# Attention products as 64x64 weights in the four quarters of the array, and float32 x of the last nine tiles for the sums of blocks

## Chip, cores and metric

The kernel runs on one core of one Trainium2 chip. The metric is the device time of one execution in microseconds (us). PE is the matrix engine (TensorE), DVE the vector engine, ACT the scalar engine, POOL the GpSimd engine, and SP the engine that issues the DMA transfers. A line number such as L895 is one of the kernel before.

## What is computed

A linear attention without softmax (4 batches, 8 heads, 576 tokens, 64 columns), then a gated feed-forward block, then a second block with a softmax-like gate and a layer norm. The sizes are 2304 tokens, 512 columns, 1536 and 1024 hidden columns.

```python
kv = einsum('bhsd,bhse->bhde', k, v)            # 64x64 for each batch and head
out = einsum('bhsd,bhde->bhse', q, kv)
x = out / sqrt(mean(out*out) + 1e-6) * g_norm   # 2304 x 512 after the heads are joined
y = ((x @ w_a) * (x @ w_b)) @ w_out             # 512 -> 1536 -> 512
h = y @ w_in                                    # 512 -> 1024
s = h * softmax(h)
result = layer_norm(s) * g_ln @ w_out2          # 1024 -> 512
```

The weights of the two blocks arrive as float64. The kernel takes each apart with integer operations and splits it into a high and a low part, and does the same with x, so that a product of near float32 accuracy is three matrix products of rounded operands.

## The kernel before

The order of all work is written by a planner that runs when the kernel is built. It keeps a clock of its own (`Order`): a step on PE has a written cost, an operation on ACT, DVE or POOL a written duration, and whatever is ready first by that clock is emitted next. Each engine then works through its list in that order and waits on the chip for what it needs. So a wait at the head of an engine's list holds all that stands behind it.

Tokens are worked in 18 tiles of 128 for the attention and in 6 blocks of 384 (three tiles each) for the first feed-forward products.

Attention. `att_kv` (L833) makes the 64x64 products k'v of a batch; ACT copies them to `bd`. `att_1` (L880) makes one tile of `out`: for each of 4 pairs of heads, 2 heads and every sequence in the tile, a product with q as the weights and `bd` as the moving operand. A sequence has 576 tokens, so tiles 4 and 13 hold two sequences and the other 16 hold one. For a tile of one sequence the weights are 64 rows by 128 columns, and there are 8 products; for a tile of two they are 64x64, and there are 16. The two heads use the upper and the lower rows of the array, and for a tile of two sequences the two halves of the tokens use the left and the right columns. After it ACT squares the tile (L933) and copies it (L935), DVE sums the squares (L923), ACT adds the epsilon, POOL takes the root, and DVE or POOL scales x (L927).

For tiles 0 to 11, `att_2` (L980) turns x on PE with four transposes; ACT writes the high part `xh` from PSUM (L994) and DVE the low part `xl` (L995). Tiles 12 to 17 go another way (`att_hop`, L939): DVE turns 32x32 blocks (L951), the tile goes to HBM and back through SP's queue (L956, L962), ACT writes a float32 tile `xs` (L965) and from it `xh` (L969), and DVE writes `xl` (L970).

First feed-forward products. `ab_items` (L1044) makes the products of the first two blocks f of 128 hidden columns, for all six blocks j of tokens: 12 units of 24 products, interleaved with the attention and then alone. The loop takes attention steps between them by a credit. Then come the "plain" units (`plain_step`, L1137) of hidden blocks 2 and 3, in three steps t of two token blocks each, 12 more units. Hidden blocks 4 to 11 are made in steps of seven products instead of eight (`step_items`, L1172), which work on sums of token blocks. `x_sums` (L1076) and `x_sum_of` (L1089) make these sums T1 to T4 for each t on DVE in PSUM banks 4 to 7 (L1098), out of the high and the low parts; T4 is written over the first half of block 2t+1, so it waits until the plain step of t is through. The sums of one t begin when those of the t before are written, and the first when all four weights of hidden blocks 2 and 3 lie in HBM.

Weights on their way: raw float64 from HBM (L381), decoded by ACT (L436) and five operations of DVE (L439 to L457), joined (L592), split (L621, L623), written to HBM (L565), and read back into their place when that is free (L686).

The names and lines that the change and the steps of the prediction touch: `w` and the loop over `bs` in `att_1` (L886 to L896), `xs_t` (L270, L948), `att_2` (L993 to L999), `SUMS`, `x_sum_of`, and the order of steps (L1703).

Of the kernel before, what the change touches and what calls it, by code (L numbers as in the profile page):

```python
# [9 lines left out]
F32 = mybir.dt.float32  # L10
F32R = mybir.dt.float32r
# [191 lines left out]
def attention_moe_moe_kernel(ctx: ExitStack, tc, kv_in, kv_tail, q_in, g_norm, w1, w_in, w_out2, g_ln, out):  # L203
# [63 lines left out]
    W_AT = [[M.W + 14336 * m + o for o in (0, 4096, 8192, 12288)] for m in range(2)]  # L267
    yb_t = [M(f"yb{i}", [P, DM], F32, W_AT[i // 2][1] + 2048 * (i % 2)) for i in range(4)]

    xs_t = [M(f"xs{i}", [P, NP, P], F32, M.R2 + 2048 * i) for i in range(6)]  # L270


    xh = [M(f"xh{j}", [P, NP, TB], F32R, M.XB + 12288 * j) for j in range(NTB)]
# [606 lines left out]
    def att_1(t):  # L880

        sx, ss, sr = (r.take() for r in (R_X, R_SQ, R_R))
        ps, free = two_banks()
        bs = seqs(t)
        off = t * P - t * P // S * S
        w = P // len(bs)  # L886
        for p in range(NP):
            if len(bs) == 2:
                src = arrived["qs", bs[0], 0][1][:, p, :]
            else:  # L890
                src = arrived["q", bs[0], p // 2][1][:, p % 2, off - (S - 4 * P) * (bs[0] % 2):][:, 0:P]
            for m, b in enumerate(bs):
                for h in range(2):
                    hs = slice(h * D, (h + 1) * D)
                    nc.tensor.matmul(ps[m * w:(m + 1) * w, h, p * D:(p + 1) * D], lhsT=src[hs, m * w:(m + 1) * w],  # L895
                                     rhs=bds[b % 2][hs, p], start=True, stop=True)  # L896
        for b in bs:
            b_left[b] -= 1
        if len(bs) == 1 and (off >= S - P or bs[0] % 2 == 0 and off == 3 * P):
            for u in range(NP // 2):  # L900
                R_Q.give(arrived.pop(("q", bs[0], u))[0])
        loads()
        x = x_t[sx % 4]
        sq = sq_t[ss % 2]
        r = r_t[sr % 4]

        o = ps[:, :, 0:NP * D].rearrange("t h (p d) -> t h p d", d=D)
        xo, sqo = (a.rearrange("t (p h) d -> t h p d", h=2) for a in (x, sq))
        rank = 1 + t / 9

        def done(when):
            R_R.give(sr)
            if t < BY_HBM:
                back.append((when, t, x, sx))
            else:
                att_hop(t, x, sx, when)

        def rest(when):
            small = ("A", 0.22, lambda: nc.scalar.activation(out=r, in_=r, func=AF.Copy, bias=1e-6))
            if t < 3:  # L920
                small = ("V", 0.1, lambda: nc.vector.tensor_scalar(out=r, in0=r, scalar1=1e-6, scalar2=None, op0=ALU.add))
            od.chain([
                ("V", 0.68, lambda: nc.vector.tensor_reduce(out=r, in_=sq, axis=AX.X, op=ALU.add)),  # L923
                (None, 0, lambda t: R_SQ.give(ss)),
                small,
                ("G", 1.76, lambda: nc.gpsimd.tensor_tensor(out=r, in0=r, in1=mhalf[:, 0:H], op=ALU.pow)),
                ("X" if t >= X_FROM else "S", (0.69, 1.3) if t >= X_FROM else 0.69, lambda e="V": tt(e)(  # L927
                    out=x, in0=x, in1=r.unsqueeze(2).to_broadcast([P, H, D]), op=ALU.mult)),
                (None, 0, done),
            ], rank=rank, t=when)  # L930

        od.chain([
            ("A", 0.6, lambda: nc.scalar.activation(out=sqo, in_=o, func=AF.Square, scale=D ** -0.5)),  # L933
            (None, 0, rest),
            ("A", 0.58, lambda: nc.scalar.copy(out=xo, in_=o)),  # L935
            free,
        ], rank=rank - 0.5, t=od.now + od.extra + 0.9 + 0.2)

    def att_hop(t, x, sx, when):  # L939

        if not R_YB.ok():
            od.chain([(None, 0, lambda w: att_hop(t, x, sx, w))], rank=1 + t / 9, t=when + 0.2)
            return
        sy = R_YB.take()
        y = yb_t[sy % 4]
        d = dr.tile([P, DM], F32, tag=f"sx{sy % 4}", name=f"sx{t}")
        dh, dl = (a[t * P // TB][:, :, t * P % TB:t * P % TB + P] for a in (xh, xl))
        xf = xs_t[t - BY_HBM]  # L948

        def turn():  # L950
            nc.vector.transpose(out=y.rearrange("t (b p i) -> t p b i", b=4, i=32),  # L951
                                in_=x.rearrange("t h d -> t (h d)").rearrange("t (p b i) -> t p b i", b=4, i=32))

        def off(when):
            R_X.give(sx)
            nc.sync.dma_start(out=d, in_=y)  # L956
            od.chain([(None, 0, back_in)], t=max(when + 2.0, od.load(4 * P * DM)))

        def back_in(when):
            assert not kv_left[0]  # L960
            for b in range(4):
                nc.sync.dma_start(out=y[b * 32:(b + 1) * 32].rearrange("i (a e) -> i a e", a=4),  # L962
                                  in_=d.rearrange("(a i) (b e) -> b i a e", a=4, b=4)[b])
            od.chain([
                ("A", 0.68, lambda: nc.scalar.activation(  # L965
                    out=xf.rearrange("c p (a j) -> c p a j", a=4), in_=y.rearrange("c (a p j) -> c p a j", a=4, p=4),
                    func=AF.Copy, scale=gn[:, 0:1])),
                (None, 0, lambda when: R_YB.give(sy)),
                ("A", 0.58, lambda: nc.scalar.copy(out=dh, in_=xf)),  # L969
                ("S", 0.64, lambda: nc.vector.tensor_tensor(out=dl, in0=xf, in1=dh.bitcast(F32), op=ALU.subtract)),  # L970
                (None, 0, ready),
            ], rank=1 + t / 9, t=max(when + 5.2, od.load(4 * P * DM) + 1.0))

        def ready(when):
            x_ready[t] = when
            att_left[0] -= 1

        od.chain([("V", 0.69, turn), (None, 0, off)], rank=1 + t / 9, t=when)

    def att_2(t, x, sx):  # L980
        ps, free = one_bank()
        xf = x.rearrange("t h d -> t (h d)")
        for p in range(NP):
            nc.tensor.transpose(ps[:, p * P:(p + 1) * P], xf[:, p * P:(p + 1) * P], ident)  # L984
        R_X.give(sx)
        src = ps.rearrange("c (p t) -> c p t", t=P)
        dh, dl = (a[t * P // TB][:, :, t * P % TB:t * P % TB + P] for a in (xh, xl))
# [1 line left out]
        def done(when):  # L989
            x_ready[t] = when  # L990
            att_left[0] -= 1

        od.chain([  # L993
            ("A", 0.68, lambda: nc.scalar.activation(out=dh, in_=src, func=AF.Copy, scale=gn[:, 0:1])),  # L994
            ("V", 0.74, lambda: nc.vector.scalar_tensor_tensor(  # L995
                out=dl, in0=src, scalar=gn[:, 0:1], in1=dh.bitcast(F32), op0=ALU.mult, op1=ALU.subtract)),
            free,
            (None, 0, done),
        ], rank=1 + t / 9, t=od.now + od.extra + 0.46 + 0.2)  # L999
    def three(o, ah, al, bh, bl, first, last, skip=False):  # L1000
        nc.tensor.matmul(o, lhsT=ah, rhs=bh, start=first, stop=False, skip_group_check=skip)  # L1001
        nc.tensor.matmul(o, lhsT=ah, rhs=bl, start=False, stop=False, skip_group_check=skip)  # L1002
# [66 lines left out]


    x_sum = {}
    SUMS = list(range(NTB // 2))
    sum_q = list(SUMS)
    sum_banks = []

# [13 lines left out]
    def x_sum_of(t):  # L1089
        i, j = 2 * t, 2 * t + 1  # L1090
        t1, t2 = PS[:, 6:8, 0:TB], PS[:, 4:6, 0:TB]
        rank = 5.075
        (b11h, b11l), (b21h, b21l) = ([a[i][:, c:c + 2] for a in (xh, xl)] for c in (0, 2))
        (b12h, b12l), (b22h, b22l) = ([a[j][:, c:c + 2] for a in (xh, xl)] for c in (0, 2))

        def add(o, a, b, op, kind="V"):
            a, b = (v.bitcast(F32) if v.dtype == F32R else v for v in (a, b))
            return (kind, 0.98, lambda: nc.vector.tensor_tensor(out=o, in0=a, in1=b, op=op))  # L1098

        def both(n, src):  # L1100
            hi, lo = (b12h, b12l) if n == T4 else [a[t][:, (T1, T2, T3).index(n)] for a in (th, tl)]
            return [("A", 0.82, lambda: nc.scalar.copy(out=hi, in_=src)), add(lo, src, hi, ALU.subtract),
                    (None, 0, lambda w: x_sum.__setitem__((t, n), w))]

        def free(*banks):
# [4 lines left out]
        def last(w):  # L1110
# [2 lines left out]
                return  # L1113
            od.chain([*both(T4, t1), *free(6, 7)], rank=rank, t=w)

        sub = ALU.subtract
        od.chain([
            add(t1, b12h, b11h, sub, "S"), add(t1, t1, b12l, ALU.add), add(t1, t1, b11l, sub), *both(T1, t1),
            add(t2, b22h, t1, sub), add(t2, t2, b22l, ALU.add), *both(T2, t2),
            add(t1, b21h, t2, sub), add(t1, t1, b21l, ALU.add), (None, 0, last),  # L1120
            add(t2, t2, b11h, sub), add(t2, t2, b11l, sub), *both(T3, t2), *free(4, 5),
        ], rank=rank, t=od.now)


    WSEQ = [("P1", 0, 0, B11), ("P6", 1, 1, T2), ("P2", 0, 1, B21), ("P5", 1, 0, T1), ("P7", 2, 0, T3),
# [11 lines left out]
    def plain_step(fp, t):  # L1137

        items = []
        last = max(t for f, t in PLAIN_STEPS if f == fp)  # L1140
        mixed = has_group(fp, 1)
        steps_left[fp, t] = 4

# [28 lines left out]
    def step_items(fp, t):  # L1172

        st = {}
        steps_left[fp, t] = 14
        left = {(m, g): (2, 2, 2, 1)[g] for m in range(2) for g in range(4)}

        def pair_of(x):
# [20 lines left out]
        def run(m, name, g, c, n):  # L1199
# [10 lines left out]
                w = wt[m][g]  # L1210
                three(ps[:, m, 0:TB], w[:, 0, sl], w[:, 1, sl], x[2 * k], x[2 * k + 1], first and k == 0, k == 1, not first)
            left[m, g] -= 1
            if not left[m, g] and t == NTB // 2 - 1:
                slot_free[m, g] = od.now
            steps_left[fp, t] -= 1
            if m:
# [483 lines left out]

    ab = [[ab_items(f, j) for j in range(NTB)] for f in range(PLAIN)]
    busy = []
    steps = [(plain_step if (fp, t) in PLAIN_STEPS else step_items)(fp, t) for fp in range(PLAIN // 2, NF1 // 2) for t in range(NTB // 2)]  # L1703
    b_items = [x for s in steps for x in s]
    ATT, LOOK = 2.0, 4

# [168 lines left out]
```

## Time and profile before

| | |
|---|---|
| median of 3 runs | 669.76 us (669.29 to 670.35) |
| the profiled execution | 670.23 us |
| its span, first to last instruction | 668.1 us |
| PE busy | 653.9 us (98%) |
| DVE, ACT, POOL busy | 503.5, 326.5, 225.4 us |

The busy time of PE is that of matmuls which overlap one another, so it tells where PE has work and not how fast it goes. A matmul of the code leaves two records in the trace, each with a weight load: 128 products of 64x128 weights stand as 256 records. A row of the timeline that ends in x16 is 16 records run together. In the chain, each piece is work that the end of the span follows from.

### The profile page before, as it was taken

To read this page: it belongs to the slowest core of one execution; us is meant where nothing else is said; L and a number is where in the kernel's file an instruction comes from. 1 tells how busy PE (TensorE), PEld (TensorE's weight loads), DVE (VectorE), ACT (ScalarE), POOL (GpSimd) and SP (SyncE) were. 2 spreads that over 40 slices of the span, in tenths; PEclk is the share of its full clock that TensorE was granted. 3 is DMA by queue.
4 is the path that set the end of the run, shared out by engine and by line. 5 is a ranking of instruction groups with operands and counts; after the bars stand their busy time and mean duration, and the time that the engine had idled before them with its cause. 6 is when DMAs were issued, how large, how long until landed. Compare 5 with 4: busy or idle time off the path is not lost.

```text
span 668.1 us, 10827 instructions
## 1 busy us (share of the span) xinstructions
PE 653.9 (98%) x3834; PEld 597.9 (89%) x3834; DVE 503.5 (75%) x784; ACT 326.5 (49%) x563; POOL 225.4 (34%) x251
## 2 busy tenths in 40 slices
PE   5999999999999999999999999999999999999998
PEld 4889998999999999999999988888888888888887
DVE  2787789888888898888478878766379996687730
ACT  3666544334544554444345444453466765564431
POOL 1575503233331330021023323111688774452100
PEclk9999999999999999999999999999999999999999
DMA  8975589558589799799975653674604565433451
GB/s 331 381 248 176 199 259 308 205 176 317 198 311 408 289 345 350 231 394 345 403 270 154 193 165 124 223 255 151 255 0 146 160 183 158 142 112 107 129 173 48
DMA packets 93654, 150.67 MB, mean 226 GB/s; under 512 B 9504, under 2 KB 60960, under 8 KB 93600
## 3 DMA queue, kind: packets, MB, share of 16 engines
q1 hardware_dynamic: 93600, 149.98, 65.2%
q8 instruction: 30, 0.49, 0.3%
q14 instruction: 24, 0.20, 0.1%
HBM read 93.33 MB, written 56.62 MB: 224 GB/s over the span
## 4 chain that ended last, share of the span: by engine, by line
PE 94%; DMA 4%; ACT 1%; DVE 1%; SPq 0%; issue 0%; ACTq 0%; DVEq 0%
PE ps L1353 22%; PE ps L1001 18%; PE ps L1002 18%; PE ps L1003 18%; PE ps L1495 13%; PE ps L895 3%; DMA hb<-stg 1%; PE ps L852 1%; DMA kv<-in_kv 1%; DMA q<-in_q 1%; DMA wt<-hb 1%; PE ps L984 1%; PE ps L860 0%; SPq L381 0%; ACT bd L866 0%
## 5 line engine op out<-in xcount | busy, mean ns | idle before, releaser
L1353 PE MATMUL ps<-gh,wo 128*128 128x512 f32 (+1 forms) x480 | 137.5, 367 | 0.0
L1001 PE MATMUL ps<-xh,wt 128*128 128x384 f32 x384 | 129.9, 338 | 2.4 <-DMA wt<-hb 1.5
L1002 PE MATMUL ps<-xl,wt 128*128 128x384 f32 x384 | 128.4, 334 | 0.0
L1003 PE MATMUL ps<-xh,wt 128*128 128x384 f32 x384 | 128.4, 334 | 0.0
L1353 PEld LDWEIGHTS ps<-gh,wo 128*128 128x128 f32 x480 | 88.8, 188 | 11.2
L1353 PE MATMUL ps<-gl,wo 128*128 128x512 f32 (+1 forms) x240 | 88.1, 367 | 0.0
L1495 PE MATMUL ps<-bo,ao 128*128 128x512 f32 x378 | 87.5, 390 | 0.0
L1495 PEld LDWEIGHTS ps<-bo,ao 128*128 128x128 f32 x378 | 70.7, 188 | 15.1 <-ACT bt L1536 0.3
L1001 PEld LDWEIGHTS ps<-xh,wt 128*128 128x128 f32 x384 | 72.1, 188 | 3.8 <-DVE tl L1098 1.8
L1327 DVE TENSOR_TENSOR gl<-gi,gh 128x512 fp32r<-128x512 f32 (+1 forms) x60 | 45.6, 767 | 37.3 <-ACT gh L1326 37.2
L1002 PEld LDWEIGHTS ps<-xl,wt 128*128 128x128 f32 x384 | 72.1, 188 | 0.1
L1003 PEld LDWEIGHTS ps<-xh,wt 128*128 128x128 f32 x384 | 72.1, 188 | 0.0
L1326 ACT CAST gh<-gi 128x512 fp32r<-128x512 f32 (+1 forms) x60 | 34.7, 580 | 74.2 <-PE ps L1353 57.6
L1002 PE MATMUL ps<-gw,dh 128*128 128x512 f32 (+1 forms) x152 | 57.4, 378 | 0.0
L1003 PE MATMUL ps<-gw,dl 128*128 128x512 f32 (+1 forms) x152 | 57.4, 378 | 0.0
L1001 PE MATMUL ps<-gw,dh 128*128 128x512 f32 (+1 forms) x152 | 57.4, 378 | 0.0
L1040 DVE TENSOR_TENSOR g<-ps,g 128x384 f32<-128x384 f32 x72 | 39.4, 553 | 21.3 <-ACT g L1039 8.4
L1039 ACT COPY g<-ps 128x384 f32<-128x384 f32 x72 | 34.0, 482 | 41.8 <-DVE ps L1249 19.5
L1353 PEld LDWEIGHTS ps<-gl,wo 128*128 128x128 f32 x240 | 45.1, 188 | 5.5
L1001 PE MATMUL ps<-th,wt 128*128 128x384 f32 x144 | 48.3, 335 | 0.2 <-ACT s L1253 0.2
L1003 PE MATMUL ps<-th,wt 128*128 128x384 f32 x144 | 48.1, 334 | 0.0
L1002 PE MATMUL ps<-tl,wt 128*128 128x384 f32 x144 | 48.1, 334 | 0.0
(127 smaller groups left out, 1225.2 us busy)
## 6 DMA issues: line engine op xcount, KB each, us to landing
raw<-in_w SPq DMA_DIRECT2D x36, 512.0 KB, 5.9
hb<-stg SPq DMA_DIRECT2D x28, 512.0 KB, 5.0
wt<-hb SPq DMA_DIRECT2D x28, 512.0 KB, 6.2
gm<-g SPq DMA_DIRECT2D x72, 192.0 KB, 4.3
gi<-gm SPq DMA_DIRECT2D x36, 256.0 KB, 2.7
su<-ya SPq DMA_DIRECT2D x34, 256.0 KB, 2.6
kv<-in_kv SPq DMA_DIRECT2D x16, 512.0 KB, 6.7
ya<-su SPq DMA_DIRECT2D x32, 256.0 KB, 3.0
```

The source lines that it names most:

```text
L852: nc.tensor.matmul(at(p)[h * D:(h + 1) * D], lhsT=k, rhs=v, start=c == 0 and p - pairs[0] < 2, stop=False, skip_group_check=True)
L895: nc.tensor.matmul(ps[m * w:(m + 1) * w, h, p * D:(p + 1) * D], lhsT=src[hs, m * w:(m + 1) * w], rhs=bds[b % 2][hs, p], start=True, stop=True)
L984: nc.tensor.transpose(ps[:, p * P:(p + 1) * P], xf[:, p * P:(p + 1) * P], ident)
L1001: nc.tensor.matmul(o, lhsT=ah, rhs=bh, start=first, stop=False, skip_group_check=skip)
L1002: nc.tensor.matmul(o, lhsT=ah, rhs=bl, start=False, stop=False, skip_group_check=skip)
L1003: nc.tensor.matmul(o, lhsT=al, rhs=bh, start=False, stop=last, skip_group_check=skip)
L1039: ("A", AC, lambda: nc.scalar.copy(out=g_t[sg], in_=ps[:, 0, 0:TB])),
L1040: ("V", VT, lambda: nc.vector.tensor_tensor(out=g_t[sg], in0=ps[:, 1, 0:TB], in1=g_t[sg], op=ALU.mult)),
L1326: ("A", 0.08 + 0.5 * k, lambda g=g, gh=gh: nc.scalar.copy(out=gh, in_=g)),
L1327: ("S", 0.08 + 0.54 * k, lambda g=g, gh=gh, gl=gl: nc.vector.tensor_tensor(out=gl, in0=g, in1=gh.bitcast(F32), op=ALU.subtract)),
L1353: nc.tensor.matmul(o, lhsT=x, rhs=y, start=f == 0 and n == 0, stop=f == NF1 - 1 and n == 2)
L1495: nc.tensor.matmul(o, lhsT=x, rhs=y, start=first and k == m == 0, stop=k == 1 and m == 2, skip_group_check=not first)
```

## The change

`att_1` cuts every tile in two halves of 64 tokens, also where both belong to one sequence. All 18 tiles then have 16 products with 64x64 weights, four of which lie in the four quarters of the array; for a tile of one sequence both column halves read the same moving operand `bd`.

For blocks 3, 4 and 5 (tiles 9 to 17), a float32 copy `xf` of the whole block is kept. It takes the place of `xs` for tiles 12 to 17. For tiles 9 to 11, `att_2` now lets ACT write `xf` from PSUM and then `xh` from `xf`, and DVE take the low part from the two in SBUF. The sums of blocks read `xf` where there is one, instead of the high and the low part one after the other. The sums are made in the order t = 2, 1, 0, and the steps of hidden blocks 2 and 3 and of 4 and 5 go in that order too, since the places of `xf` are later written over by sums.

```diff
-    xs_t = [M(f"xs{i}", [P, NP, P], F32, M.R2 + 2048 * i) for i in range(6)]
+    XF_AT = {3: M.T0 + 6144, 4: M.R2, 5: M.R2 + 6144}
+    xf_t = {j: M(f"xf{j}", [P, NP, TB], F32, at) for j, at in XF_AT.items()}
...
-        w = P // len(bs)
+        w = P // 2
...
-            for m, b in enumerate(bs):
+            for m, b in enumerate((bs[0], bs[-1])):
                 for h in range(2):
                     hs = slice(h * D, (h + 1) * D)
                     nc.tensor.matmul(ps[m * w:(m + 1) * w, h, p * D:(p + 1) * D], lhsT=src[hs, m * w:(m + 1) * w],
...
-        xf = xs_t[t - BY_HBM]
+        xf = xf_t[t * P // TB][:, :, t * P % TB:t * P % TB + P]
...
+        if j in xf_t:
+            xf = xf_t[j][:, :, t * P % TB:t * P % TB + P]
+            ops = [
+                ("A", 0.68, lambda: nc.scalar.activation(out=xf, in_=src, func=AF.Copy, scale=gn[:, 0:1])),
+                free,
+                ("A", 0.58, lambda: nc.scalar.copy(out=dh, in_=xf)),
+                ("S", 0.64, lambda: nc.vector.tensor_tensor(out=dl, in0=xf, in1=dh.bitcast(F32), op=ALU.subtract)),
+            ]
...
-    SUMS = list(range(NTB // 2))
+    SUMS = [2, 1, 0]
+    T_ORDER = {PLAIN // 2: SUMS, PLAIN // 2 + 1: SUMS}
...
+        (b11, b21), (b12, b22) = ([[xf_t[n][:, c:c + 2]] if n in xf_t else [a[n][:, c:c + 2].bitcast(F32) for a in (xh, xl)]
+                                   for c in (0, 2)] for n in (i, j))
...
+        def minus(o, x, y):
+            return [op(o, x[0], y[0], sub, "S")] + [op(o, o, p, add) for p in x[1:]] + [op(o, o, p, sub) for p in y[1:]]
+
+        def less(o, x, s):
+            return [op(o, x[0], s, sub)] + [op(o, o, p, add) for p in x[1:]]
...
-        od.chain([
-            add(t1, b12h, b11h, sub, "S"), add(t1, t1, b12l, ALU.add), add(t1, t1, b11l, sub), *both(T1, t1),
-            add(t2, b22h, t1, sub), add(t2, t2, b22l, ALU.add), *both(T2, t2),
-            add(t1, b21h, t2, sub), add(t1, t1, b21l, ALU.add), (None, 0, last),
-            add(t2, t2, b11h, sub), add(t2, t2, b11l, sub), *both(T3, t2), *free(4, 5),
-        ], rank=rank, t=od.now)
+        ops = [*minus(t1, b12, b11), *both(T1, t1), *less(t2, b22, t1)]
+        if j in xf_t:
+            ops += [*minus(t1, b22, b12), *both(T2, t2), *both(T3, t1), *less(t1, b21, t2), *free(4, 5), (None, 0, last)]
+        else:
+            ops += [*both(T2, t2), *less(t1, b21, t2), (None, 0, last)]
+            ops += [op(t2, t2, p, sub) for p in b11] + [*both(T3, t2), *free(4, 5)]
+        od.chain(ops, rank=rank, t=od.now)
...
-    steps = [(plain_step if (fp, t) in PLAIN_STEPS else step_items)(fp, t) for fp in range(PLAIN // 2, NF1 // 2) for t in range(NTB // 2)]
+    steps = [(plain_step if (fp, t) in PLAIN_STEPS else step_items)(fp, t) for fp in range(PLAIN // 2, NF1 // 2) for t in T_ORDER.get(fp, range(NTB // 2))]
```

## Rows read from the trace of the kernel before

**Rows 1.** The page: busy time, share of the span, instructions of each engine.
```profile
PE 653.9 (98%) x3834; PEld 597.9 (89%) x3834; DVE 503.5 (75%) x784; ACT 326.5 (49%) x563; POOL 225.4 (34%) x251
```

**Rows 2.** Waits of PE: line, releaser, us in total, times, longest.
```profile
PE ps L852 <- DMA kv<-in_kv: 7.3, 3, 4.1
PE ps L1001 <- DMA wt<-hb: 1.5, 1, 1.5
PE ps L1001 <- ACT s L1230: 0.9, 1, 0.9
```

**Rows 3.** The chain in order of time: start us, us, what.
```profile
13.90 7.61 PE ps L895 x64
...
48.42 1.93 PE ps L895 x32
...
58.68 0.62 PE ps L895 x32
...
62.58 1.04 PE ps L895 x16
```

**Rows 4.** L895 in three windows: duration ns min/median/max, first and last start, form.
```profile
L895 PE MATMUL ps<-bd,q x16: 417/418/473, 13.8 to 15.8; 64*128 64x64 f32 x16
L895 PE MATMUL ps<-bd,qs x32: 218/218/267, 27.4 to 27.8; 64*64 64x64 f32 x32
L895 PE MATMUL ps<-bd,q x16: 272/272/320, 28.6 to 29.4; 64*128 64x64 f32 x16
```

**Rows 5.** Windows: stretch; PE, PEld, DVE, ACT, POOL busy (records); PEclk; DMA; GB/s.
```profile
13.80:21.50 7.70, 7.70 (x68) 7.46 (x66) 4.04 (x9) 4.31 (x9) 3.16 (x2) 1.00 1.01 375
21.50:30.40 8.90, 8.64 (x146) 7.40 (x145) 6.71 (x12) 6.32 (x15) 6.26 (x5) 1.00 1.06 383
21.50:103.00 81.50, 80.93 (x832) 75.84 (x832) 66.34 (x114) 49.07 (x104) 38.92 (x27) 1.00 0.72 251
103.00:116.00 13.00, 11.48 (x65) 10.90 (x64) 12.29 (x19) 5.09 (x10) 3.94 (x5) 1.00 0.91 302
116.00:170.00 54.00, 52.93 (x304) 52.29 (x303) 47.17 (x69) 21.88 (x38) 18.19 (x19) 1.00 0.63 224
170.00:332.00 162.00, 162.00 (x936) 161.81 (x935) 133.59 (x237) 75.57 (x133) 30.88 (x30) 1.00 0.90 330
```

**Rows 6.** Timeline of ACT: start, us, instruction, idle before and its releaser.
```profile
15.50 0.66 ACT L436 ACTIVATE u<-raw 128x512 f32<-128x512 f32 x1 [1.12 <-DMA raw<-in_w]
16.43 0.60 ACT L933 ACTIVATE sq<-ps 128x512 f32<-128x512 f32 x1 [0.28 <-PE ps L895]
...
18.63 1.07 ACT L935 COPY x<-ps 128x512 f32<-128x512 f32 x2
```

**Rows 7.** Timeline of DVE: low parts of tiles 2 and 17, and a product.
```profile
29.84 0.75 DVE L995 SCALAR_TENSOR_TENSOR xl<-ps,gn,xh 128x512 fp32r<-128x512 f32 x1
...
92.46 0.68 DVE L970 TENSOR_TENSOR xl<-xs,xh 128x512 fp32r<-128x512 f32 x1
...
99.39 0.56 DVE L1040 TENSOR_TENSOR g<-ps,g 128x384 f32<-128x384 f32 x1 [0.80 <-PE ps L1003]
```

**Rows 8.** The chain from 102 us: the write, reading and first use of a weight.
```profile
102.50 8.67 DMA hb<-stg
111.23 4.27 DMA wt<-hb
115.63 0.41 PE ps L1001
```

**Rows 9.** L1098, the sums, on DVE: duration ns min/median/max, first and last start, form.
```profile
L1098 DVE TENSOR_TENSOR ps<-ps,xl x15: 955/956/967, 105.4 to 165.8; 128x768 f32<-128x768 f32 x15
```

**Rows 10.** The copies of tiles 12 to 17 out of `xs`: ACT, then DVE.
```profile
L969 ACT CAST xh<-xs x6: 617/622/623, 76.9 to 91.7; 128x512 fp32r<-128x512 f32 x6
L970 DVE TENSOR_TENSOR xl<-xs,xh x6: 649/684/686, 79.7 to 92.5; 128x512 fp32r<-128x512 f32 x6
```

**Rows 11.** Timeline of PE: first products with the first and the last token block.
```profile
30.36 0.42 PE L1001 MATMUL ps<-xh,wt 128*128 128x384 f32 x1
...
94.96 0.33 PE L1001 MATMUL ps<-xh,wt 128*128 128x384 f32 x1
```

More of the change, by code (lines that the diff above doesn't have):

```diff
@@ L981, in att_2 @@
         ps, free = one_bank()
-        xf = x.rearrange("t h d -> t (h d)")
+        xo = x.rearrange("t h d -> t (h d)")
         for p in range(NP):
-            nc.tensor.transpose(ps[:, p * P:(p + 1) * P], xf[:, p * P:(p + 1) * P], ident)
+            nc.tensor.transpose(ps[:, p * P:(p + 1) * P], xo[:, p * P:(p + 1) * P], ident)
         R_X.give(sx)
@@ L991, in done @@
             att_left[0] -= 1
-        od.chain([
[L994 to L999, printed above, removed]
+        j = t * P // TB
+        if j in xf_t:
[7 more added lines that the diff above has]
+        else:
+            ops = [
+                ("A", 0.68, lambda: nc.scalar.activation(out=dh, in_=src, func=AF.Copy, scale=gn[:, 0:1])),
+                ("V", 0.74, lambda: nc.vector.scalar_tensor_tensor(
+                    out=dl, in0=src, scalar=gn[:, 0:1], in1=dh.bitcast(F32), op0=ALU.mult, op1=ALU.subtract)),
+                free,
+            ]
+        od.chain([*ops, (None, 0, done)], rank=1 + t / 9, t=od.now + od.extra + 0.46 + 0.2)
     def three(o, ah, al, bh, bl, first, last, skip=False):
@@ L1092, in x_sum_of, with op @@
         rank = 5.075
[L1093 to L1098, printed above, removed]
+        h12, l12 = (a[j][:, 0:2] for a in (xh, xl))
+        (b11, b21), (b12, b22) = ([[xf_t[n][:, c:c + 2]] if n in xf_t else [a[n][:, c:c + 2].bitcast(F32) for a in (xh, xl)]
+                                   for c in (0, 2)] for n in (i, j))
+        add, sub = ALU.add, ALU.subtract
+        def op(o, a, b, what, kind="V"):
+            return (kind, 0.98, lambda: nc.vector.tensor_tensor(out=o, in0=a, in1=b, op=what))
+        def minus(o, x, y):
+            return [op(o, x[0], y[0], sub, "S")] + [op(o, o, p, add) for p in x[1:]] + [op(o, o, p, sub) for p in y[1:]]
+        def less(o, x, s):
+            return [op(o, x[0], s, sub)] + [op(o, o, p, add) for p in x[1:]]
         def both(n, src):
-            hi, lo = (b12h, b12l) if n == T4 else [a[t][:, (T1, T2, T3).index(n)] for a in (th, tl)]
-            return [("A", 0.82, lambda: nc.scalar.copy(out=hi, in_=src)), add(lo, src, hi, ALU.subtract),
+            hi, lo = (h12, l12) if n == T4 else [a[t][:, (T1, T2, T3).index(n)] for a in (th, tl)]
+            return [("A", 0.82, lambda: nc.scalar.copy(out=hi, in_=src)), op(lo, src, hi.bitcast(F32), sub),
                     (None, 0, lambda w: x_sum.__setitem__((t, n), w))]
@@ L1114, in last @@
             od.chain([*both(T4, t1), *free(6, 7)], rank=rank, t=w)
-        sub = ALU.subtract
-        od.chain([
-            add(t1, b12h, b11h, sub, "S"), add(t1, t1, b12l, ALU.add), add(t1, t1, b11l, sub), *both(T1, t1),
-            add(t2, b22h, t1, sub), add(t2, t2, b22l, ALU.add), *both(T2, t2),
-            add(t1, b21h, t2, sub), add(t1, t1, b21l, ALU.add), (None, 0, last),
-            add(t2, t2, b11h, sub), add(t2, t2, b11l, sub), *both(T3, t2), *free(4, 5),
-        ], rank=rank, t=od.now)
+        ops = [*minus(t1, b12, b11), *both(T1, t1), *less(t2, b22, t1)]
+        if j in xf_t:
+            ops += [*minus(t1, b22, b12), *both(T2, t2), *both(T3, t1), *less(t1, b21, t2), *free(4, 5), (None, 0, last)]
+        else:
+            ops += [*both(T2, t2), *less(t1, b21, t2), (None, 0, last)]
+            ops += [op(t2, t2, p, sub) for p in b11] + [*both(T3, t2), *free(4, 5)]
+        od.chain(ops, rank=rank, t=od.now)
     WSEQ = [("P1", 0, 0, B11), ("P6", 1, 1, T2), ("P2", 0, 1, B21), ("P5", 1, 0, T1), ("P7", 2, 0, T3),
@@ L1139, in plain_step @@
         items = []
-        last = max(t for f, t in PLAIN_STEPS if f == fp)
+        last = [t for t in T_ORDER.get(fp, range(NTB // 2)) if (fp, t) in PLAIN_STEPS][-1]
         mixed = has_group(fp, 1)
@@ L1175, in step_items @@
         steps_left[fp, t] = 14
+        last = T_ORDER.get(fp, range(NTB // 2))[-1]
         left = {(m, g): (2, 2, 2, 1)[g] for m in range(2) for g in range(4)}
@@ L1212, in run @@
             left[m, g] -= 1
-            if not left[m, g] and t == NTB // 2 - 1:
+            if not left[m, g] and t == last:
                 slot_free[m, g] = od.now
```

## The prediction

> **What bounds the kernel now.** I read the page's busy times first: PE is busy for 653.9 of 668.1 us [rows 1]. So microseconds taken from PE's list are worth something, unless PE then waits for them. The waits of PE come second [rows 2]: 7.3 us for the first k and v, before any attention tile; then 1.5 us for a weight read back from HBM and 0.9 us for ACT in the first steps on sums. From 170 to 332 us the list is dense [rows 5]. Third comes the cover. DVE is busy for 66.3 of 81.5 us from 21.5 to 103, and for 12.3 of the 13 us after it [rows 5]. It is nearly as full as PE, and it feeds PE through x and through the decoded weights. The question is therefore not whether PE's attention gets shorter, but how much of that DVE and the transfers can follow.
>
> **Part 1: the products of attention.** The trace before holds both forms, since two of the 18 tiles hold two sequences. At full pace a tile of one sequence is a piece of 1.04 us with 16 records, a tile of two is a piece of 0.62 us with 32 records, each with what it costs to enter and leave that form [rows 3]. By starts, 16 records of 64x128 spread over 0.8 us and 32 of 64x64 over 0.4 us [rows 4]. So the difference is 0.42 us either way. Twelve tiles of one sequence run at that pace (5 to 12 and 14 to 17): 12 x 0.42 = **5.0 us off PE's list**. Tiles 4 and 13 do not change.
>
> Tiles 0 to 3 run before 21.5 us at a slower pace: 7.61 us for 64 records, 1.90 per tile, and a record takes 418 ns where the same form later takes 272 [rows 3, 4]. The granted clock of that window is given as 1.00, the 2.4 GHz level, as it is later [rows 5]; the durations say otherwise, and I go by the durations. Two such tiles in a row later take 1.93 us, 0.965 each [rows 3], so the slow pace is 1.90 / 0.965 = 1.97 times the other. No row shows a 64x64 tile at that pace in a dense row of them. Bounds: no gain at all, and 4 x 1.97 x 0.45 (only the spread of the starts) = 3.5 us, a gain of 4.1. I take 4 x 1.97 x 0.62 = 4.9 us, a gain of **2.7 us**, since the 0.62 is a whole tile.
>
> Can that gain be used at once? ACT squares and copies each tile. Its first square stands behind the decode of a weight that waits for a DMA until 15.50 us and ends at 16.16; the square now starts at 16.43 [rows 6], so little is lost there. Two of ACT's operations run in 1.07 us, so a tile costs ACT about 1.07, less than the 1.22 that PE would need. Next come the products of batch 1 and its q. That q is issued when tile 3 is through, and the DMA engines are full (1.01 and 1.06 of their time [rows 5]), so tile 5 may wait a little: I put 0.3 us back. The first feed-forward unit at 30.36 already starts as DVE finishes `xl` of tile 2, at 30.59 [rows 7, 11]; DVE is idle for 2.2 us between 21.5 and 30.4 [rows 5], so it can follow by about that. Net of this place: -2.4 us.
>
> A rule of the Trainium skill speaks against this part. "TensorE: Matmul & The Clock Gate" (Wait — 56ns, not 53.3ns?) says that starts of matmuls are never closer than about 25 ns, however small they are. By it, 32 records would need 0.80 us, and the twelve tiles would give an estimated 12 x 0.24 = 2.9 us. The row does not agree: 32 records fit in 0.62 us, 19 ns each, with entry and exit [rows 3].
>
> **Part 2: x of tiles 9 to 11.** Before, ACT writes `xh` and DVE `xl` from PSUM. Now ACT does one operation more, as for tiles 12 to 17 (0.62 us), and DVE one of 0.68 in place of 0.75 [rows 7, 10]. That is 3 x 0.62 = 1.9 us more of ACT, which is busy for 49.1 of 81.5 us there [rows 5], and nothing on DVE; the PSUM bank comes free earlier. On the path it is nothing, hidden behind the feed-forward units between the tiles; without that cover, 0.6 us for each tile. The copies of tiles 12 to 17 only change their place in memory.
>
> **Part 3: the sums.** By the code, one t has 13 operations on DVE (9 for the sums, 4 for the low parts), 39 in all, 0.956 us each [rows 9]. After the change t = 2 has 8, t = 1 has 10, t = 0 has 13: 31. So DVE loses 8 x 0.956 = 7.6 us, nearly all after 103 us, and the short ones come first. None of it is on PE's list. What it is worth: from 116 to 170 DVE is busy for 47.2 of 54 us, and PE loses 54 - 52.9 = 1.1 us, most of it to ACT and DVE [rows 2, 5]. I take 0.7 of these back, with bounds of 0 and 1.1. The new order t = 2, 1, 0 moves whole steps of equal length; T4 of the first t waits for its own plain step as before. The weights of hidden blocks 4 and 5, which DVE decodes between the sums, come earlier, as they must, because PE will ask for them earlier.
>
> **The place that takes some back.** At 115.63 PE has waited 1.5 us for the last weight of hidden blocks 2 and 3. This weight left DVE at 102.5, took 8.67 us to HBM and 4.27 us back [rows 2, 8]. PE will come there 5.0 + 2.4 = 7.4 us earlier. Does the weight? Before it, DVE stands at 99.39 waiting for PE's product [rows 7], so part of its pace is PE's own. But its 66.3 us of work from 21.5 to 103 would have to fit in 81.5 - 7.4 = 74.1, a share of 0.90, in a list with a fixed order. Bounds: it follows fully (0), or not at all (7.4 given back). I take 2.0: at 0.90 it follows with most, not all. A second place hangs on the same lag: the last token block is ready at 93.1 and used at 94.96 [rows 7, 11], 1.8 us of slack. A lag of 2 us costs no more there, since the same time would be spent waiting for the weight.
>
> **Sum**, against the profiled execution of 670.23 us: -5.0 - 2.4 - 0.7 + 2.0 = -6.1, so 664.1. The profiled run lies 0.5 above the median of 669.76; the same offset gives **663.7 us**.
>
> **The rivals**, all in medians.
> (a) *The weights set the pace.* The weight at 115 comes when it came before, and the whole lead of 7.4 us turns into waiting there; only the 0.7 remain: 669.0. For it: DVE is full just there (12.3 of 13 us), and the DMA engines are at 0.91 [rows 5]. Against it: DVE's own waits for PE in the stretch before. Chance 0.16.
> (b) *What follows the products sets the pace in the first 30 us.* A tile needs DVE for a reduction, a scaling and a low part, beside the decode, and DVE has 6.7 of 8.9 us to do from 21.5 to 30.4 [rows 5]. If the first unit still starts near 30.3, the 2.4 us of the first tiles are lost: 663.7 + 2.4 = 666.1. The Trainium skill, "TensorEngine Tiling (Array Packing)" (PSUM Bottleneck), says that tiling speeds up the array but not the emptying of PSUM, which may become the bound; by that rule this case would hold. The trace bears it out in part only: ACT's 1.07 us for a tile lie under PE's 1.22, by 0.15 [rows 6]. Chance 0.17.
> (c) *The quarters take turns.* In tiles 4 and 13 the two column halves read two different `bd`; in the other tiles both will read the same rows at the same addresses, and no row of before shows that. If left and right wait for each other, a tile is 16 products in turn of two: 2 x 1.04 us, scaled by 218 / 272 for the smaller form [rows 3, 4], are 1.67, so +0.63 for each of twelve tiles and 1.97 times that for the first four, 7.6 + 5.0. That gives 669.8 + 12.6, about 682. It decides where a record takes more than 1.04 / 32 = 33 ns. Against it: records in separate quarters ran at 19 ns. This is also how the change might not do what it says. Chance 0.06.
> (d) *The long wait slows PE.* In case (a) the gap at 115 would be 1.5 + 7.4 = 8.9 us, far over the longest after 25 us in the trace. If PE comes out of it at the pace of the first tiles for as long as their dense 7.6 us [rows 3], half of that is lost: 669.0 + 3.8 = 672.8. Chance 0.03.
>
> **How the numbers follow.** The forecast has 0.58, (a) 0.16, (b) 0.17, (c) 0.06, (d) 0.03. The best sum of the bounds is -5.0 - 3.8 - 1.1 + 0 = -9.9, 659.9; the forecast with a lag of 0 to 4 us instead of 2 gives 661.7 to 665.7. The range is 660.4 to 668.8: it takes in (b), most of the bounds, and the cases in which the weight gives back up to 7 us, short of the full (a). About 0.2%, 1.3 us, is what a measurement can tell from no change. Faster: the forecast, (b) and some of (a), 0.82. Within: the rest of (a), 0.09. Slower: (c) and (d), 0.09.
>
> **What would show each step.** L895 with 576 records, all 64x64; 0.62 us for a tile in the chain after 25 us, and about 1.2 before it. The first feed-forward unit near 28 us. The last attention tile near 65 us instead of 72. A wait for `wt<-hb` near 110 us, 3.5 us by the forecast and 9 by (a). Thirty-one sums' operations on DVE. Fewer waits of PE for ACT between 150 and 170 us. From 170 us on the same list, shifted. The prediction is wrong if a 64x64 tile of one sequence takes over 1 us, if the weights come no earlier, or if the new order puts a wait where none was.

## The result and the profile after

The changed kernel takes 663.25 us (median of 4 runs, 661.30 to 664.61) against 669.75 us (4 runs, 669.29 to 670.35). The ratio is 0.990, with a 95% interval of 0.9872 to 0.9929. The forecast was 663.7 us. The profiled execution took 662.49 us with a span of 660.7; that of before took 670.23 and 668.1.

The page of the changed kernel, first part: busy time, share, instructions.

```profile
PE 644.6 (98%) x4090; PEld 589.3 (89%) x4090; DVE 498.9 (76%) x788; ACT 328.2 (50%) x566; POOL 218.3 (33%) x239
```

PE has 9.3 us less to do than in [rows 1], with 256 records more: the 128 products that the change adds (a product of the attention leaves two records, one of the feed-forward units a single one). DVE has 4.6 us less, and not the 7.6 that the sums alone were to take from it. The planner may give the splitting and joining of weights and the scaling of x to DVE or to POOL, and after the change twelve more of these operations stand on DVE: POOL went from 251 to 239 instructions, DVE from 784 to 788 in spite of the 8 that the sums lost. The chain in order of time (start, us, what) shows what the first feed-forward unit follows from, the tiles in their new form, and the weight that PE waits for near 110 us.

```profile
15.79 0.68 ACT u L438
...
18.73 2.04 POOL r L928
...
23.43 3.47 POOL r L928 x2
26.93 1.61 DVE x L929
28.58 0.65 PE ps L986 x4
31.43 1.09 PE ps L897 x64
...
46.34 1.09 PE ps L897 x64
...
59.24 0.62 PE ps L897 x32
60.60 0.62 PE ps L897 x32
66.63 0.62 PE ps L897 x32
...
96.86 7.69 DMA hb<-stg
104.69 5.20 DMA wt<-hb
```

Where the chain before has PE's own products for 7.61 us from 13.9 us on [rows 3], it now goes over a weight's decoding on ACT, POOL's roots and DVE's scaling of x. A tile of one sequence is now a piece of 0.62 us with 32 records, and two in a row take 1.09, against 1.04 and 1.93 in [rows 3]. The difference is 0.42 us, as counted. The timeline of PE from 14 us (start, us, line, records, idle before and its releaser) shows the first tiles and what PE waits for between them. L897 is the attention product, L986 the transposes, L1013 the first product of a feed-forward unit.

```profile
14.73 2.83 PE L897 MATMUL ps<-bd,q 64*64 64x64 f32 x94 [0.52 <-ACT bd L868]
18.10 1.13 PE L897 MATMUL ps<-bd,q 64*64 64x64 f32 x32 [0.54 <-ACT x L937]
...
27.43 0.46 PE L897 MATMUL ps<-bd,q 64*64 64x64 f32 x16 [0.53 <-DMA q<-in_q]
28.58 0.65 PE L986 MATMUL ps<-ident,x 128*128 128x128 f32 x4 [0.69 <-DVE x L929]
29.00 0.42 PE L1013 MATMUL ps<-xh,wt 128*128 128x384 f32 x1
...
42.07 0.46 PE L897 MATMUL ps<-bd,q 64*64 64x64 f32 x16 [0.94 <-DMA q<-in_q]
```

All waits of PE after the change, to be read against [rows 2] and against two further waits of the kernel before, which stand first:

```profile
PE ps L895 <- DMA q<-in_q: 0.3, 1, 0.3
PE ps L984 <- DVE x L927: 0.3, 1, 0.3
...
PE ps L854 <- DMA kv<-in_kv: 7.6, 3, 4.4
PE ps L897 <- DMA q<-in_q: 1.5, 2, 0.9
PE ps L1013 <- DMA wt<-hb: 1.1, 1, 1.1
PE ps L986 <- DVE x L929: 0.9, 2, 0.7
PE ps L897 <- ACT x L937: 0.5, 1, 0.5
PE ps L897 <- ACT bd L868: 0.5, 1, 0.5
PE ps L854 <- ACT bd L868: 0.5, 1, 0.5
```

The waits in the attention have grown: 1.5 us instead of 0.3 for q, 0.9 instead of 0.3 for x from DVE, and 0.5 for ACT's copy out of PSUM, which is new. The wait for the weight is 1.1 instead of 1.5 us, and the wait for ACT in the first steps on sums (0.9 us for L1230 in [rows 2]) is gone. In windows (columns as in [rows 5]):

```profile
21.50:30.40 8.90, 7.47 (x132) 6.14 (x128) 8.43 (x14) 6.84 (x16) 5.43 (x4) 1.00 1.06 394
21.50:103.00 81.50, 78.87 (x1015) 73.66 (x1012) 70.51 (x122) 51.64 (x109) 35.33 (x23) 1.00 0.79 274
103.00:116.00 13.00, 11.88 (x70) 11.59 (x68) 10.60 (x21) 5.12 (x9) 3.70 (x4) 1.00 0.82 296
116.00:170.00 54.00, 54.00 (x311) 53.63 (x311) 48.73 (x78) 23.02 (x41) 12.96 (x12) 1.00 0.73 246
```

DVE went from 6.71 to 8.43 of 8.90 us between 21.5 and 30.4 us, so it became the full engine there, and PE has holes. From 116 to 170 us PE no longer has any.

The clearest reading is the start of the same piece of work in each kernel. The starts below are read from the timelines of PE, at each first product of a unit of 24 products; in brackets stands the lead over the kernel before. The last columns are experiments of the next section.

| start of | before | after | attention only | sums only | sums from high and low | four places for q |
|---|---|---|---|---|---|---|
| first unit | 30.36 | 29.00 (1.36) | 28.95 (1.41) | 30.63 (-0.27) | 28.90 (1.46) | 28.94 (1.42) |
| first unit after the last attention tile | 78.32 | 73.33 (4.99) | 73.26 (5.06) | 78.69 (-0.37) | 72.58 (5.74) | 72.08 (6.24) |
| first plain unit | 103.28 | 98.34 (4.94) | 98.65 (4.63) | 103.73 (-0.45) | 97.73 (5.55) | 97.22 (6.06) |
| unit behind the last weight of hidden blocks 2 and 3 | 117.79 | 112.19 (5.60) | 113.57 (4.22) | 116.93 (0.86) | 110.94 (6.85) | 113.79 (4.00) |
| fourth of the units on sums | 169.33 | 162.40 (6.93) | 165.12 (4.21) | 167.17 (2.16) | 163.81 (5.52) | 164.95 (4.38) |
| a unit of hidden blocks 6 and 7 | 223.41 | 216.48 (6.93) | 219.20 (4.21) | 221.25 (2.16) | 221.40 (2.01) | 219.03 (4.38) |

The lead of the changed kernel is 5.0 us when attention is over, 5.6 behind the weight, 6.9 behind the first steps on sums, and stays there until 284 us. The rest of the 7.4 us between the spans comes later in small pieces.

### The profile page after: what moved, and what is told of

It reads as the page before. It is cut to its first block, busy times and chain, and to the rows that moved or that the text cites. A ratio compares the mean times of both kernels' runs of the same rounds, so it can differ in the third digit from the quotient of the medians.

```text
span 660.7 us, 11343 instructions
## 1 busy us (share of the span) xinstructions
PE 644.6 (98%) x4090; PEld 589.3 (89%) x4090; DVE 498.9 (76%) x788; ACT 328.2 (50%) x566; POOL 218.3 (33%) x239
## 4 chain that ended last, share of the span: by engine, by line
PE 88%; DMA 6%; DVE 2%; SPq 1%; POOL 1%; ACT 1%; issue 1%; ACTq 0%; DVEq 0%
PE ps L1377 22%; PE ps L1013 17%; PE ps L1014 17%; PE ps L1015 17%; PE ps L1519 13%; DMA raw<-in_w 1%; DMA hb<-stg 1%; PE ps L897 1%; DMA kv<-in_kv 1%; DMA q<-in_q 1%; POOL r L928 1%; DMA wt<-hb 1%; SPq L964 1%; DMA yb<-sx 1%; DVE x L929 1%
## 5 line engine op out<-in xcount | busy, mean ns | idle before, releaser
L1013 PE MATMUL ps<-xh,wt 128*128 128x384 f32 x384 | 129.8, 338 | 1.1 <-DMA wt<-hb 1.1
L1013 PEld LDWEIGHTS ps<-xh,wt 128*128 128x128 f32 x384 | 72.1, 188 | 2.1 <-DVE ws L646 1.4
L1013 PE MATMUL ps<-gw,dh 128*128 128x512 f32 (+1 forms) x152 | 57.4, 378 | 0.0
L1273 DVE TENSOR_TENSOR ps<-ps,s 128x768 f32<-128x768 f32 x36 | 34.7, 964 | 20.0 <-PE ps L1015 20.0
L594 POOL TENSOR_TENSOR f<-f,u 128x512 f32<-128x512 f32 x12 | 16.2, 1346 | 97.6 <-DVE u L459 67.5
L1013 PE MATMUL ps<-th,wt 128*128 128x384 f32 x144 | 48.2, 335 | 0.0
```

Of the source, the lines that this page charges most:

```text
L594: od.chain([("X", (0.62, 1.32), lambda e: tt(e)(out=f, in0=f, in1=u_t[su], op=ALU.add)), (None, 0, have)], rank=rank_of(k), t=t)
L1273: return ("V", 2 * VT - 0.15, lambda: nc.vector.tensor_tensor(out=o, in0=a, in1=b, op=ALU.add))
```

## Experiments

**The parts alone: the products.** The kernel before with only this edit:

```diff
-        w = P // len(bs)
+        w = P // 2
...
-            for m, b in enumerate(bs):
+            for m, b in enumerate((bs[0], bs[-1])):
```

> The kernel before with the 64x64 products alone; x, the sums and their order stay as before. Theory (the parts add up: the products give 5 us by the end of the attention, the sums 1.3 us more near 160 us): about 664.8 us, the plain units begin at 98.3 as in the changed kernel, the wait for the weight at 110 stays between 1 and 2 us, and the waits of PE for ACT and DVE between 155 and 165 us stay at 1.1 us or grow to 2. Rival (the lighter sums are what lets the weights and the sums keep up with an earlier PE): the lead of 5 us is given back by 2 us or more after 103 us, so 667 us or more.

It took 665.59 us (5 runs, 664.29 to 666.02), 0.9932 of before (0.9917 to 0.9946), so 3.9 us less. The forecast of 664.8 was a little too good, and the rival's 667 was not reached. Its timeline of PE shows where the lead of 5.06 us went:

```profile
98.65 0.41 PE L1001 MATMUL ps<-xh,wt 128*128 128x384 f32 x1 [0.27 <-DMA wt<-hb]
102.55 0.41 PE L1001 MATMUL ps<-xh,wt 128*128 128x384 f32 x1 [1.55 <-DMA wt<-hb]
111.41 0.41 PE L1001 MATMUL ps<-xh,wt 128*128 128x384 f32 x1 [0.27 <-DMA wt<-hb]
...
157.60 0.44 PE L1001 MATMUL ps<-th,wt 128*128 128x384 f32 x1 [0.18 <-ACT s L1253]
162.93 0.45 PE L1001 MATMUL ps<-xh,wt 128*128 128x384 f32 x1 [0.89 <-ACT s L1230]
```

The weights of hidden blocks 2 and 3 take part of it back, now at 98.6 and 102.5 already, and the two waits for ACT in the steps on sums are those of before, to the hundredth. The products alone bring a lead of 4.2 us, which stands unchanged from 114 to 219 us.

**The parts alone: the sums.** The changed kernel with the two lines of the last diff turned back.

> The changed kernel with the attention products as before (64x128 weights for tiles of one sequence); float32 x, the sums and the order t = 2, 1, 0 as in the changed kernel. Theory (parts add up): about 668.4 us; the attention ends as in the kernel before, the plain units begin near 103.3, and the 1.1 us of waits between 160 and 168 us are gone. Rival (the lighter sums matter only for an earlier PE): 669.5 to 670 us, no change.

It took 667.32 us (5 runs, 667.13 to 668.28), 0.9966 (0.9953 to 0.9979): 2.2 us less than before, with no earlier attention at all. So the rival falls, and the theory's 1.3 was too small. The table shows two equal steps of 1.3 us: at the weight, where PE waits 0.4 instead of 1.5 us, and in the first steps on sums, where the waits for ACT are gone. The first of these steps does not come from operations that the sums lost: the first sum starts at 102.11 us, and the weight's write begins at 102.25, hardly earlier than the 102.50 of before. Its write took 7.6 us instead of 8.67; why is open. Against the 669.49 us of the kernel before beside these runs (16 runs), the two parts alone add up to 6.1 us; together they gave 6.5 in the result, and 6.6 by the medians of a second series (662.66 below, against 669.21).

**The sums again from two parts.** The changed kernel with the new order and the float32 copies, but with sums as before:

```diff
-        (b11, b21), (b12, b22) = ([[xf_t[n][:, c:c + 2]] if n in xf_t else [a[n][:, c:c + 2].bitcast(F32) for a in (xh, xl)]
+        (b11, b21), (b12, b22) = ([[a[n][:, c:c + 2].bitcast(F32) for a in (xh, xl)]
                                    for c in (0, 2)] for n in (i, j))
...
-        if j in xf_t:
+        if False:
             ops += [*minus(t1, b22, b12), ...]
```

> The changed kernel, with the sums again made out of the high and the low parts (39 operations of DVE instead of 31), in the order t = 2, 1, 0. Theory (the 8 operations less are what frees PE near 160 us): about 664.5 to 665.5 us, with waits of PE for ACT or DVE of 1 to 2 us between 110 and 170 us. Rival (the new order alone does it): 663.2 us and no such waits.

It took 667.81 us (11 runs, 666.61 to 670.65), 0.9977 (0.9965 to 0.999), only 1.7 us less than before, and so gives back most of the gain, more than either theory said. Behind the last weight of hidden blocks 2 and 3 it has the largest lead of that row, 6.85 us. Then its timeline of PE has these waits:

```profile
154.28 0.41 PE L1013 MATMUL ps<-th,wt 128*128 128x384 f32 x1 [1.45 <-DMA wt<-hb]
...
163.81 0.44 PE L1013 MATMUL ps<-xh,wt 128*128 128x384 f32 x1 [0.96 <-DVE ps L1273]
...
203.18 0.44 PE L1013 MATMUL ps<-th,wt 128*128 128x384 f32 x1 [1.65 <-DMA wt<-hb]
206.44 0.44 PE L1013 MATMUL ps<-th,wt 128*128 128x384 f32 x1 [0.90 <-ACT s L1277]
```

By the last row of the table the lead is 2.0. The waits are for weights that DVE decodes between the sums, for DVE itself, and for ACT. So in the new order the sums of 39 operations lose 4.8 us of lead, and the shorter sums keep it. This holds for the new order only: with the products alone there are 39 operations too, in the order t = 0, 1, 2, and a lead of 4.2 us loses nothing over the same stretch. Why the new order needs the shorter sums, and whether a lead of 6.85 us would have lasted in the old one, was not tried.

**The first four tiles as before.** The changed kernel with

```diff
-        w = P // 2
+        two = [bs[0], bs[-1]] if t > 3 else bs
+        w = P // len(two)
...
-            for m, b in enumerate((bs[0], bs[-1])):
+            for m, b in enumerate(two):
```

> The changed kernel, with tiles 0 to 3 made by 64x128 weights as before and the rest by 64x64. By the prediction's working the first four tiles are worth 2.4 us: 665.6 us. By the trace of the changed kernel the first feed-forward unit comes only 1.4 us earlier, or 1.7 if the later arrival of k and v in that execution is counted: 664.8 us. Rival (the DMA transfers of q and DVE hold that stretch anyway, and the clock of PE rises later): within 0.5 us of the changed kernel, 663.2 to 663.7.

It took 664.16 us (5 runs, 663.51 to 665.0), 0.9919 (0.9905 to 0.9933). Against the medians of the changed kernel, 663.25 and 662.66, that is 0.9 to 1.5 us, but the intervals overlap (0.9872 to 0.9929 for the changed kernel), and the times alone exclude neither 0 nor 2.4. They depend on the granted clock as well: all five executions here have a mean of 1.000, and the four of the changed kernel with 0.999 or 1.000 (660.54 to 662.49) lie 2.3 us lower by their medians. The trace says less: the first unit starts at 29.72 instead of 29.00, and the first unit after the last attention tile at 73.45 instead of 73.33, because the wait for q in tile 9 is 0.32 instead of 0.94 us. So 0.7 us of lead comes out of the first four tiles here, and most of it is gone by the end of the attention; what they are worth in time is not settled.

**Four places for q.** In the changed kernel the loads of q for batch b+1 wait until the tiles of batch b have read theirs. Two more places, in memory that the sums use later, take that wait away:

```diff
-    q_t = [M(f"q{i}", [P, 2, 4 * P], F32, M.R2 + 18432 + 4096 * i) for i in range(2)]
+    q_t = [M(f"q{i}", [P, 2, 4 * P], F32, at) for i, at in enumerate((M.R2 + 18432, M.R2 + 22528, M.T0, M.T0 + 12288))]
...
-    R_KV, R_TAIL, R_Q, RAW = Ring(4), Ring(1), Ring(2), Slots(3)
+    R_KV, R_TAIL, R_Q, RAW = Ring(4), Ring(1), Ring(4), Slots(3)
...
-                t = q_t[slot % 2]
+                t = q_t[slot % 4]
```

> The changed kernel with four places for q instead of two (the two new ones lie in memory that the sums use later), so that the loads of q no longer wait for the tiles before. In the changed kernel PE waits 0.5 us for q before tile 5 and 0.9 before the second half of tile 9. Theory (the place of q holds these loads back and takes part of what the 64x64 products give): both waits are gone, the plain units begin about 1 us earlier than 98.3, and the time is 662.0 to 662.5 us. Rival (the DMA engines are full there, so q comes when it came, or something else comes later): no change, 663.2 us, with the waits at other transfers.

The changed kernel ran beside it once more:

> The changed kernel once more, beside the next two on the same chip: 662.5 to 664 us, with the granted clock at 1.000 in some executions and about 0.997 in others.

That took 662.66 us (6 runs, 660.54 to 667.27), and the kernel with four places 662.33 us (6 runs, 659.83 to 665.72). The two can't be told apart by time. The traces can: the waits for q are gone, and the lead after the attention is 6.24 us instead of 4.99, as the theory said. But all of that and more is lost at one place in the profiled execution, which with 665.72 us is the slowest of the six. First the timeline of PE, then two windows (stretch; PE busy, records; PEclk; DMA; GB/s):

```profile
110.97 0.41 PE L1013 MATMUL ps<-xh,wt 128*128 128x384 f32 x1 [3.08 <-DMA wt<-hb]
...
112.83 0.52 PE L1013 MATMUL ps<-xh,wt 128*128 128x384 f32 x1
...
112.00:114.00 2.00, 2.00 (x9) 0.59 0.09 37
114.00:116.00 2.00, 2.00 (x8) 0.56 0.26 92
```

Two things happen there. The weight left DVE 6.3 us earlier than before (its write begins at 96.18 and not at 102.50), about as much as PE's lead of 6.1; but write and reading back took 7.91 and 6.61 us, 14.5 together, instead of 12.9 both before and after the change. So what the wait has over the 1.49 us of before comes from the two transfers of this execution, not from DVE, and the lead falls to 4.66. After the hole of 3.08 us the granted clock is at 1.2 GHz for some 3 us, a product takes 0.52 us instead of 0.33, and the lead is down to 3.06 by 123.05 us; the 4.00 of the table stands in the middle of that. The shorter waits in the steps on sums then bring 1.3 back. Whether the other five executions lose anything here is not known.

**Four places for q and the first four tiles as before.**

> Four places for q, and tiles 0 to 3 with 64x128 weights as before. Tells apart what makes the granted clock fall in some executions. Theory (PE's waits in the 64x64 products of the first four tiles, between 14 and 30 us, let the clock fall for some 3 us in some executions): the clock is 0.999 or 1.000 in every execution, the executions lie within 1.5 us, and the median is 663 to 663.5 us. Rival (any earlier attention does it): clocks of 0.997 here too, as often as in the changed kernel.

It took 662.66 us (5 runs, 662.54 to 664.2), 0.9903 (0.9886 to 0.992): as fast as the changed kernel by its median and a little better than the theory's time, with a spread of 1.7 us instead of 3.3 and 6.7. The mean granted clock of its five executions was 1.000, 1.000, 1.000, 0.999 and 0.999, as the theory said; with four places and 64x64 products in the first tiles five of six had 0.997. None of these kernels is clearly faster than the changed one.

## Why the prediction was right

The time was forecast within 0.5 us, but that closeness is luck: the mechanism was right, two of its terms were not, and their errors cancelled. The products gave 2.4 us less than forecast by the end of the attention, and the weight, which was to take 2.0 back, gave 0.7. For the profiled execution the forecast was 664.1 us, and 662.49 was measured.

*The products at full pace.* The step from 1.04 to 0.62 us for a tile was right. Of the twelve tiles, one runs before the first unit; the other eleven are worth 11 x 0.42 = 4.6 us, and the lead grew by 4.99 - 1.36 = 3.6. The missing microsecond is the wait for q in the middle of tile 9, 0.94 us instead of 0.3, and waits for x. The prediction put 0.3 us on q, and only for tile 5. The load of q is issued when the last tile of the batch before is through, and its flight does not shrink (5.32 us before, 5.85 after); with less work of PE beside it, more of it shows. The kernel with four places bears this out: without that wait the lead is 6.24.

*The first four tiles.* Forecast -2.4 us, measured 1.4 by the first unit, with the 0.42 of tile 5 in it, and 0.7 by the experiment's first unit. The products themselves became even shorter than taken: 94 records in 2.83 us are 0.96 us for a tile at the slow pace, not 1.22. What failed was the step on who follows. At 0.96 us PE is under ACT's 1.07 for a tile, and waits 0.54 us for its copy out of PSUM before tile 3. Then q (0.53) and x from DVE (0.69) hold it, while DVE is busy for 8.43 of 8.90 us. The prediction let DVE follow by its 2.2 idle microseconds and had no price for POOL, whose roots stand in the chain with 2.04 and 3.47 us just before that x. So rival (b) came half true. The rule of the Trainium skill that stood beside it ("TensorEngine Tiling (Array Packing)", PSUM Bottleneck) agrees with one wait of these four tiles, the 0.54 us. Part of that wait is ACT's late start: its first square stands behind the decode of a weight, which ends at 16.47 us in the chain, as before the change. For the tiles between feed-forward units no wait of PE names ACT. The 25 ns that the Trainium skill gives as the least distance between starts ("TensorE: Matmul & The Clock Gate", Wait — 56ns, not 53.3ns?) do not hold for the records here: 64 records take 1.09 us, 17 ns each. Counted by the products of the code, which leave two records each, it is 34 ns.

*The weight at 115 us.* Forecast +2.0, measured -0.7: the lead grew there from 4.94 to 5.60. This is the largest error in the sum. The weight left DVE at 96.86 instead of 102.50, 5.6 us earlier, so DVE followed fully and a little more: between 21.5 and 103 us its idle time went from 15.2 to 11.0 us. Write and reading back together took what they took before: 7.69 and 5.20 us instead of 8.67 and 4.27. With the products alone, the place took 0.8 net out of 5.06; with the sums alone it gave 1.3. The prediction asked only whether DVE follows and held the two transfers constant. In the five profiles whose chain shows this weight's transfers the write took from 7.6 to 9.4 us and the reading from 3.5 to 6.6, and in the kernel with four places for q they, and not DVE, made the wait twice as long.

*The sums.* Forecast 31 operations and 0.7 us. The trace has 31 records on the line of the sums, of 0.95 us each; the first of them, with both operands in float32, and the two longest groups are

```profile
L1113 DVE TENSOR_TENSOR tl<-ps,th x9: 945/952/958, 100.6 to 158.9; 128x768 fp32r<-128x768 f32 x9
L1113 DVE TENSOR_TENSOR ps<-ps,xl x7: 953/957/961, 121.2 to 157.1; 128x768 f32<-128x768 f32 x7
...
L1113 DVE TENSOR_TENSOR ps<-xf,xf x1: 965/965/965, 97.1 to 97.1; 128x768 f32<-128x768 f32 x1
```

The waits between 155 and 168 us are gone to the last tenth: 6.93 - 5.60 = 1.33 us, the bound I gave, and a little over it. What the prediction missed is the value of the shorter sums for the lead itself, once the order is changed. It said that the new order "moves whole steps of equal length" and that the weights of hidden blocks 4 and 5 "come earlier, as they must", and put no price on either; the kernel with the sums from two parts lost 4.8 us of lead between 150 and 223 us, and the products alone, in the old order, lost none there.

*The rivals.* (a) did not happen: the weight came 5.6 us earlier. That DVE could follow because PE's own products had paced its list is argued from its idle time, 4.2 us less while the lead grew to 4.9. (c) is excluded: two quarters that read the same rows of `bd` run at 17 to 19 ns a record, as those that read different ones. (d) did not happen in the changed kernel's profile, but its mechanism did at that very place with four places for q, after a hole of 3.08 us and not 8.9: the clock cost 1.6 us there.

The sum with the measured terms: 5.0 us up to the end of the attention, 0.6 at the weight, 1.3 in the steps on sums, 0.5 in small pieces after that, together 7.4 us between the spans, where the forecast had 6.1.

## What to carry to other kernels

Where one engine is busy for 98%, taking work from it pays only as far as its suppliers can follow; price each supplier's flight time that the removed work used to cover, above all loads that are issued only when a buffer comes free. Ask of a new order of work by itself what it costs the supplier: here the two parts alone gave 3.9 and 2.2 us, which nearly add up, but the first part in the second's order of work, without its shorter sums, kept only 1.7. Read the lead at marked pieces of work, not the total, to see where time is won and given back.

## What the runs showed of the hardware that was not expected

The changed kernel scatters over 3.3 us in 4 runs (6.7 in 6 runs of the second series), where the kernel before stays within 3.1 us in 16 runs and 3.6 in 11. Part of the reason is the granted clock: the four executions with a mean of 0.999 or more took 660.54 to 662.49 us, the six below it 661.91 to 667.27. In the second series' profile of the changed kernel, the windows of PE (stretch; PE busy, records; PEclk; DMA; GB/s) are

```profile
17.00:19.00 2.00, 1.51 (x56) 1.00 1.06 359
19.00:21.00 2.00, 1.16 (x28) 1.00 1.01 391
21.00:23.00 2.00, 1.68 (x40) 1.00 1.08 329
23.00:25.00 2.00, 1.51 (x46) 1.00 1.06 408
25.00:27.00 2.00, 1.05 (x20) 1.00 1.05 395
27.00:29.00 2.00, 1.28 (x18) 0.70 1.01 407
29.00:31.00 2.00, 2.00 (x9) 0.50 1.04 418
31.00:33.00 2.00, 2.00 (x38) 0.95 1.02 411
```

The clock falls to 0.50 (1.2 GHz) for some 3 us, just as the feed-forward units begin. Before it fell PE had been busy for 1.05 to 1.68 us of each window, and from 14 us on no single wait was over 1.14 us. The first unit starts 0.4 us later than in the execution shown above, and the second, behind the slow stretch, 1.2 us later. With four places for q one such stretch cost 1.6 us of lead, so it alone does not explain a scatter of 6.7. The durations of a 64x64 record in the same execution tell both levels:

```profile
L897 PE MATMUL ps<-bd,q x32: 218/218/267, 17.8 to 18.3; 64*64 64x64 f32 x32
L897 PE MATMUL ps<-bd,q x16: 311/312/365, 27.7 to 28.4; 64*64 64x64 f32 x16
```

The first line also shows that PE can reach its full pace already at 17.8 us, in the fourth tile of 64x64 products; with 64x128 products the same tiles stay at 418 ns a record up to 21.1 us, and the pace rises near 25. Of the five profiled executions with 64x64 products in the first four tiles, two have all of the fourth tile at 218 ns (this one and that of the products alone), and in these two the clock falls near 27.5 us; in the other three some or all records of that tile take 311 ns, and the clock does not fall there. The lower clock goes with the form of the first four tiles: of the executions with 64x64 products there (five series), 21 of 32 have a mean clock below 0.999; of the 15 with 64x128 products there and the rest of the change or a part of it (three series), none, and of the kernel before 1 of 27. A mean does not tell where the clock fell: with four places for q the profiled execution has its slow stretch at 112 us, behind the wait for a weight. So the 64x64 form of the first four tiles brings lower means and more scatter, while its gain is not settled. That the holes are what lets the clock fall was not tried by itself and stays argued.
